# Linear attention and two squared-ReLU FFNs on one core: weights at multiples of 512 bytes, activations 64 bytes past one

## Chip, cores and metric

One core of a Trainium2 chip runs one program. The time is the device time of an execution in microseconds; of a kernel it is the median of its runs. The profiled execution is one more run, with its own time.

## What is computed

The reference, cut to its core. Everything is float32, with 8 x 576 = 4,608 tokens, 8 heads of 64, a model width of 512 and a hidden width of 2,048:

```python
q_s = exp(q - q.max(-1)); q_s = q_s / (q_s.sum(-1) + 1e-9)          # over the head's 64 columns
k_s = exp(k - k.max(2));  k_s = k_s / (k_s.sum(2) + 1e-9)            # over the 576 positions
kv = einsum('bhsd,bhse->bhde', k_s, v)
x = einsum('bhsd,bhde->bhse', q_s, kv)                               # laid out as [4608, 512]
x = square(maximum(x @ moe_w_in, 0)) @ moe_w_out
y = square(maximum(x @ moe2_w_in, 0)) @ moe2_w_out
```

## The kernel before, in words

The tokens are cut into nine blocks j of 512. TensorE works through four phases, each over all nine blocks before the next begins.

Phase 0 (up to 514 us): the attention gives x of a block, transposed, in four tiles [128, 512] (`x_mm`, lines 360 to 368), and `h_mm` (line 383) multiplies it by w_in of the first FFN. A product is done in float32r with both operands split into a high and a low part, three passes for each (`passes`, line 400; the matmul is line 404). A chunk of 128 hidden columns takes 4 x 3 = 12 matmuls of 128x128 weights by 512 columns; a block has 16 chunks.

Phase 1 (514 to 874 us), `second_mm` with l = 0 (line 461): the second product of the first FFN. It is done in the seven products of a Strassen scheme: `combine` (line 641) makes of a tile of weights or of activations seven linear combinations of its quarters, on VectorE and GpSimd (`comb_add`, lines 82 to 86), splits them into a high part on ScalarE (line 92) and a low part on VectorE (line 97), and puts both into one tile [128, 2, 7, 256]. A step a (eight to a block) takes seven products by two halves by three passes, 42 matmuls of 256 columns, with one tile of weights W and one of activations G.

Phase 2 (874 to 1247 us), `first_mm` (line 413): the first product of the second FFN in the same scheme, 84 matmuls of 256 columns for each of four units u of a block, with two tiles W and two tiles x.

Phase 3 (1247 us to the end), `second_mm` with l = 1: as phase 1, but `left, right = (w, g) if l == 0 else (g, w)` (line 466) turns the operands round. `nc.tensor.matmul(ps, a, b)` loads a (128 columns, LDWEIGHTS in the profile) and streams b. So in phases 0 to 2 the weights are loaded and the activations stream; in phase 3 G is loaded and W streams.

Each matmul of line 404 loads weights of its own, and the load for the next matmul runs while the present one streams.

SBUF is divided into places. A tile belongs to a tag, a tag has one buffer (`tile_pool(name="sb", bufs=1)`, line 53), and tiles of one tag follow each other in it. The tags that the change touches are w0 to w7 and hl0 to hl3, each 14 x 256 float32 (14,336 bytes) in every partition:

- w0 to w4 hold in phase 0 three chunks each of the split w_in (line 701: `w0_rooms`), with the chunks f = 0 to 2 in w0, 3 to 5 in w1 and so on. The last chunk, f = 15, lies in hl3. From phase 1 on, w0 to w7 hold the eight tiles W of a phase: step a uses w((a + 5) mod 8) (`slot_of`, line 719). In phase 2 unit u uses two of them.
- hl0 and hl1 hold in phase 0 three of the four tiles x of even and of odd blocks; the fourth lies in hl3 (line 827). In phases 1 and 3, G of step n = 8j + a lies in hl((n + 1) mod 3) (line 947), but for the last steps, which use two places. In phase 2 the two tiles x of a block lie in hl3 and hl0 or in hl1 and hl2.

All slices that a matmul takes of these tiles begin at multiples of 512 bytes from the tile's start.

The order of the work on each engine is fixed before the program is built: `schedule` (line 556) runs a model of the five engines with estimated costs and due times, and the steps are issued in the order that it gives. It knows tags, not addresses. Where a tag lies is settled by the order in which the tags first get a tile: the pool puts them one behind another, rounded up to 32 bytes, from byte 1,152 of a partition.

Of the kernel before, what the change touches and what calls it, by code (L numbers as in the profile page):

```python
# [8 lines left out]
F32 = mybir.dt.float32  # L9
# [11 lines left out]
P = 128  # L21
NP = H // 2
TB = 512
HB = TB // 2
# [17 lines left out]
def linear_attention_two_relu2_ffn(ctx: ExitStack, tc: tile.TileContext, q0, k0, eye, qh, kh, vh, wio, out):  # L42
# [10 lines left out]
    pool = ctx.enter_context(tc.tile_pool(name="sb", bufs=1))  # L53
    psum = ctx.enter_context(tc.tile_pool(name="ps", bufs=1, space=bass.MemoryType.PSUM))
    dram = ctx.enter_context(tc.tile_pool(name="dr", bufs=1, space=bass.MemoryType.DRAM))

    def f32(ap):
        return ap.bitcast(F32)
# [1022 lines left out]
```

## Time and profile before

| | |
|---|---|
| median of 3 runs | 1610.74 us (1606.44 to 1611.1) |
| the profiled execution's own time | 1609.91 us |
| its span, first to last instruction | 1608.1 us |
| TensorE busy (matmul) | 1558.7 us, 97% |
| VectorE busy | 1210.4 us, 75% |
| ScalarE busy | 960.7 us, 60% |
| GpSimd busy | 414.3 us, 26% |
| mean granted clock of TensorE | 0.989 |
| matmuls of line 404, 512 columns in phase 0 | 1,728 |
| matmuls of line 404, 256 columns in phases 1 to 3 | 3 x 3,024 |

A busy share says that an engine has something in flight, not that it works at its best: matmuls are pipelined, and the 280 or so ns that the profile gives for one are the time from its start to its end, of which more than half overlaps the next. What a matmul costs is the distance from its start to the next start. In a stretch in which TensorE is busy from end to end, that is the stretch divided by the number of matmuls.

### The profile page before, as it was taken

What the parts mean: (1) busy time and instruction counts of PE and PEld (TensorE: products, weight loads), DVE (VectorE), ACT (ScalarE), POOL (GpSimd) and SP (SyncE); (2) the same over time, 40 slices, a digit from 0 to 9 for tenths busy, and PEclk for the clock granted to TensorE, in tenths of its full rate; (3) what the DMA queues carried; (4) which work ended last, traced back from release to release, by engine and by line L of the source; (5) the groups of instructions that cost most, each with busy time, mean ns of one, the idle gap of its engine ahead of it and who ended that gap; (6) DMA issues with size and microseconds to landing.
All of it is one profiled execution on the core that took longest, in us unless ns stands there. A gap on an engine that the chain in (4) does not pass through costs nothing. (4 is left out here: it accounts for less than half of the span.)

```text
span 1608.1 us, 29959 instructions
## 1 busy us (share of the span) xinstructions
PE 1558.7 (97%) x11664; PEld 1458.2 (91%) x11664; DVE 1210.4 (75%) x1758; ACT 960.7 (60%) x1605; POOL 414.3 (26%) x329
## 2 busy tenths in 40 slices
PE   5889999999999999999999899999999999999998
PEld 4668887778888999999999899999999999999998
DVE  7887886777632988888889854544337999999986
ACT  7666775666643655555556677777668543434432
POOL 1000000000013333333322243333311533333332
PEclk9899999999999999999999899999999999999999
DMA  8536775677655333333334466665335443333332
GB/s 320 166 119 220 243 252 187 224 240 226 196 183 176 139 132 130 133 132 132 131 111 157 162 214 192 207 207 175 131 132 190 152 144 136 134 134 136 132 118 80
DMA packets 139135, 270.50 MB, mean 168 GB/s; under 512 B 12144, under 2 KB 71664, under 8 KB 138992
## 3 DMA queue, kind: packets, MB, share of 16 engines
q1 hardware_dynamic: 138992, 268.58, 50.3%
q8 instruction: 91, 1.49, 0.4%
q14 instruction: 52, 0.43, 0.1%
HBM read 161.58 MB, written 106.95 MB: 167 GB/s over the span
## 5 line engine op out<-in xcount | busy, mean ns | idle before, releaser
L404 PE MATMUL h<-hl,w 128*128 128x512 f32 x1620 | 399.3, 401 | 13.2 <-DVE w L64 12.1
L404 PEld LDWEIGHTS h<-hl,w 128*128 128x128 f32 x1620 | 305.4, 191 | 84.6 <-DVE w L64 10.9
L404 PE MATMUL m<-x,W 128*128 128x256 f32 x3024 | 362.5, 283 | 6.7 <-DVE W L97 6.4
L404 PEld LDWEIGHTS m<-x,W 128*128 128x128 f32 x3024 | 361.4, 190 | 7.5 <-DVE W L97 7.0
L404 PE MATMUL y<-W,G 128*128 128x256 f32 x3024 | 355.7, 280 | 4.6 <-DVE G L97 4.6
L404 PE MATMUL y<-G,W 128*128 128x256 f32 x3024 | 358.6, 281 | 1.2 <-DVE G L97 1.2
L404 PEld LDWEIGHTS y<-G,W 128*128 128x128 f32 x3024 | 358.2, 189 | 1.7 <-DVE G L97 1.6
L404 PEld LDWEIGHTS y<-W,G 128*128 128x128 f32 x3024 | 354.6, 188 | 5.4 <-DVE G L97 4.6
L92 ACT ACTIVATE G<-hl 128x512 fp32r<-128x512 f32 (+1 forms) x106 | 93.3, 888 | 139.1 <-PE y L404 104.3
L97 DVE TENSOR_TENSOR G<-hl,G 128x512 fp32r<-128x512 f32 (+1 forms) x106 | 128.7, 1218 | 17.8 <-ACT G L92 17.7
L391 ACT ACTIVATE r<-h 128x512 f32<-128x512 f32 x144 | 85.3, 594 | 74.7 <-PE h L404 69.9
L434 POOL TENSOR_TENSOR ts<-ts,ts 128x512 f32<-128x512 f32 x53 | 79.7, 1504 | 183.4 <-ACT ts L431 171.0
L443 DVE TENSOR_TENSOR t<-m,ts 128x512 f32<-128x512 f32 x72 | 49.4, 689 | 100.3 <-PE m L404 89.1
L258 POOL PARTITION_ALL_REDUCE m<-m x28 | 23.4, 836 | 348.2 <-DVE m L254 155.0
L449 ACT ACTIVATE t<-t 128x512 f32<-128x512 f32 x144 | 90.3, 631 | 3.6
L97 DVE TENSOR_TENSOR G<-cf,G 128x1280 fp32r<-128x1280 f32 x51 | 84.8, 1662 | 4.4 <-ACT G L92 4.1
L97 DVE TENSOR_TENSOR G<-att,G 128x1280 fp32r<-128x1280 f32 x50 | 82.2, 1644 | 6.0 <-ACT G L92 5.8
L92 ACT ACTIVATE G<-qd 128x512 fp32r<-128x512 f32 x40 | 25.3, 632 | 80.8 <-PE y L404 59.0
L92 ACT ACTIVATE G<-cf 128x1280 fp32r<-128x1280 f32 x51 | 64.5, 1265 | 14.7 <-DVE cf L84 11.6
L92 ACT ACTIVATE G<-att 128x1280 fp32r<-128x1280 f32 x50 | 63.2, 1265 | 16.1 <-DVE att L84 16.0
L92 ACT ACTIVATE G<-qc 128x512 fp32r<-128x512 f32 x41 | 25.9, 632 | 76.1 <-PE y L404 69.3
L476 POOL TENSOR_TENSOR t<-t,t 128x512 f32<-128x512 f32 x34 | 62.9, 1870 | 30.1 <-DVE t L443 30.1
(166 smaller groups left out, 1988.2 us busy)
## 6 DMA issues: line engine op xcount, KB each, us to landing
g<-r SPq DMA_DIRECT2D x144, 256.0 KB, 3.3
g<-t SPq DMA_DIRECT2D x144, 256.0 KB, 2.7
hl<-g SPq DMA_DIRECT2D x63, 512.0 KB, 3.6
raw<-wio SPq DMA_DIRECT2D x48, 512.0 KB, 5.1
qc<-g SPq DMA_DIRECT2D x41, 512.0 KB, 3.6
qd<-g SPq DMA_DIRECT2D x40, 512.0 KB, 3.6
y<-t SPq DMA_DIRECT2D x72, 256.0 KB, 2.2
w<-wf SPq DMA_DIRECT2D x48, 256.0 KB, 5.0
```

The source lines that it names most:

```text
L92: nc.scalar.activation(out=hls[key][:, 0, r], in_=src, func=AF.Copy)
L97: nc.vector.tensor_tensor(out=hl[:, 1, r], in0=src, in1=f32(hl[:, 0, r]), op=ALU.subtract)
L258: nc.gpsimd.partition_all_reduce(m[:, 1, :P], m[:, 0, :P], P, bass.bass_isa.ReduceOp.max)
L391: nc.scalar.activation(out=r0[j, f].rearrange("p a b -> p (a b)"), in_=m.pop(("h", j, f)), func=AF.Relu)
L404: nc.tensor.matmul(ps, a, b, start=start, stop=True, skip_group_check=True)
L434: nc.gpsimd.tensor_tensor(out=t[k, "s5"], in0=t[k, "s5"], in1=t[k, "s2"], op=ALU.add)
L443: nc.vector.tensor_tensor(out=temp(k, q), in0=m[k, i], in1=t[k, "s5"], op=ALU.add)
L449: nc.scalar.activation(out=t[k, q], in_=t[k, q], func=AF.Square)
L476: nc.gpsimd.tensor_tensor(out=t[k, q], in0=t[k, q], in1=t[k, o], op=ALU.add)
```

## The change

Before any other tile is asked for, the pool is asked for one tile of each of fourteen tags in a fixed order, which settles where these tags lie. Nothing writes or reads these first tiles. The lines behind move down by eight (line 404 becomes 412).

```diff
     pool = ctx.enter_context(tc.tile_pool(name="sb", bufs=1))
     psum = ctx.enter_context(tc.tile_pool(name="ps", bufs=1, space=bass.MemoryType.PSUM))
     dram = ctx.enter_context(tc.tile_pool(name="dr", bufs=1, space=bass.MemoryType.DRAM))
+
+
+    pool.tile([P, 224], F32, name="margin", tag="margin")
+    for tag in [f"w{i}" for i in range(8)]:
+        pool.tile([P, 14 * HB], F32, name=f"{tag}_room", tag=tag)
+    pool.tile([P, 16], F32, name="margin2", tag="margin2")
+    for tag in [f"hl{i}" for i in range(4)]:
+        pool.tile([P, 14 * HB], F32, name=f"{tag}_room", tag=tag)
```

Where the built programs put the places, in bytes from the start of a partition, with the remainder by 512:

| place | before | mod 512 | after | mod 512 |
|---|---|---|---|---|
| w0 | 116,416 | 192 | 2,048 | 0 |
| w1 | 155,392 | 256 | 16,384 | 0 |
| w2 | 175,936 | 320 | 30,720 | 0 |
| w3 | 9,344 | 128 | 45,056 | 0 |
| w4 | 23,680 | 128 | 59,392 | 0 |
| w5, w6, w7 | 38,112, 52,448, 66,784 | 224 | 73,728, 88,064, 102,400 | 0 |
| hl0 | 100,032 | 192 | 116,800 | 64 |
| hl1 | 190,272 | 320 | 131,136 | 64 |
| hl2 | 213,824 | 320 | 145,472 | 64 |
| hl3 | 136,896 | 192 | 159,808 | 64 |

The other places move as well: the eight 2,048-byte places of the evictions from 192 or 256 to 128 or 192 past a multiple of 512, qc and cf from 320 to 256, att2 from 352 to 288, qd from 128 to 64. The instructions of all five engines, their order and their waits are the same, row for row.

## Rows read from the trace of the kernel before

**Rows 1.** The page's head and its first part.
```profile
span 1608.1 us, 29959 instructions
...
PE 1558.7 (97%) x11664; PEld 1458.2 (91%) x11664; DVE 1210.4 (75%) x1758; ACT 960.7 (60%) x1605; POOL 414.3 (26%) x329
```

**Rows 2.** The page's second part: busy tenths in 40 slices of some 40 us.
```profile
PE   5889999999999999999999899999999999999998
...
DVE  7887886777632988888889854544337999999986
...
PEclk9899999999999999999999899999999999999999
```

**Rows 3.** Waits of ScalarE from 1300 to 1590 us: total, times, longest.
```profile
ACT G L92 <- PE y L404: 100.0, 36, 4.4
```

**Rows 4.** Timeline of TensorE, opening of phase 3: start, length, count, idle before.
```profile
1297.72 2.52 PE L404 MATMUL y<-W,G 128*128 128x256 f32 x19 [1.57 <-DVE G L97]
```

**Rows 5.** Stretches of phase 1: length, TensorE busy, matmuls, clock, DMA share, GB/s.
```profile
690.54:695.57 5.03, 5.03 (x44) 1.00 0.41 134
695.57:700.52 4.95, 4.95 (x44) 1.00 0.51 175
705.57:710.33 4.76, 4.76 (x44) 1.00 0.32 110
710.33:715.28 4.95, 4.95 (x44) 1.00 0.34 121
```

**Rows 6.** Stretches of phase 3, the same view.
```profile
1435.68:1440.45 4.78, 4.78 (x44) 1.00 0.41 148
1440.45:1445.21 4.76, 4.76 (x44) 1.00 0.36 120
...
1464.97:1469.92 4.94, 4.94 (x44) 1.00 0.58 202
1469.92:1474.94 5.02, 5.02 (x44) 1.00 0.21 65
1474.94:1479.89 4.95, 4.95 (x44) 1.00 0.42 147
1479.89:1484.65 4.76, 4.76 (x44) 1.00 0.34 119
```

**Rows 7.** Stretches of phase 0, one chunk each, the same view.
```profile
295.47:298.27 2.80, 2.80 (x14) 1.00 0.86 222
473.08:475.80 2.72, 2.72 (x13) 1.00 0.70 215
481.32:484.12 2.80, 2.80 (x13) 1.00 0.48 113
486.92:489.71 2.79, 2.79 (x13) 1.00 0.23 86
500.79:503.54 2.75, 2.75 (x13) 1.00 0.27 105
```

**Rows 8.** Tile G from 1300 to 1590 us: nanoseconds least/median/most, first and last start.
```profile
L97 DVE TENSOR_TENSOR G<-cf,G x20: 1475/1489/2206, 1303.2 to 1580.2; 128x1280 fp32r<-128x1280 f32 x20
...
L97 DVE TENSOR_TENSOR G<-att,G x20: 1477/1487/2206, 1309.9 to 1585.2; 128x1280 fp32r<-128x1280 f32 x20
```

**Rows 9.** Stretches by engine: length, busy (count) of PE, PEld, DVE, ACT, POOL, clock, DMA.
```profile
530.00:860.00 330.00, 330.00 (x2788) 330.00 (x2788) 287.78 (x311) 193.53 (x217) 110.08 (x89) 1.00 0.38 132
...
1247.00:1300.00 53.00, 48.36 (x406) 47.58 (x405) 50.27 (x59) 25.55 (x30) 29.27 (x14) 1.00 0.49 150
1300.00:1590.00 290.00, 290.00 (x2481) 290.00 (x2480) 261.12 (x273) 116.47 (x132) 103.29 (x79) 1.00 0.38 130
```

**Rows 10.** Stretches of phase 2: two blocks, and one of hl3, hl0 with w3, w4.
```profile
1041.82:1121.20 79.38, 79.38 (x674) 1.00 0.61 193
1077.10:1081.34 4.24, 4.24 (x38) 1.00 0.31 103
```

## The prediction, made before the changed kernel ran

> **What bounds the kernel now.** I read the head of the page first: the span is 1608.1 us and TensorE is busy for 97% of it [rows 1]. The slices then show where that holds: from the fourth slice on TensorE stands at 9 with one 8 in the middle, its clock is granted in full nearly throughout, and the only engine near it is VectorE, at 8 and 9 through much of the second quarter and nearly all of the last [rows 2]. In phase 3 the feeders wait for TensorE and not the reverse: ScalarE sat 100.0 us idle, 36 times, until a matmul had released a place hl [rows 3]. Only at the opening of phase 3 does TensorE wait for VectorE's G, in stalls such as 1.57 us [rows 4]. So the time is, to first order, the number of matmuls times the distance between two starts, and the question is whether that distance depends on where the operands lie.
>
> It does, already in the kernel before. Call D the start of the moving operand minus the start of the weights that are loaded next, modulo 512 bytes; within a tile all operands of the three FFN phases and of phase 0 start at multiples of 512 bytes, so D is a property of the two places. In phases 1 and 3 one pair of places is used for 42 matmuls on end, and the stretches in the rows run from the first start of one pair to the first start of the next (a count of x44 holds the two neighbours that overlap the edges). The clock is 1.00 in all of them and TensorE is busy from end to end, so nothing but the pair differs. Phase 1 [rows 5]: hl0 with w0 (D 0) takes 5.03 us, hl1 with w1 (D 64) 4.95, hl0 with w3 (D 64) 4.76, hl1 with w4 (D 192) 4.95. Per matmul that is 119.8, 117.8, 113.4 and 117.8 ns. Phase 3, where the weights move and G is loaded [rows 6]: w3 past hl0 (D 448) 4.78 us, w4 past hl1 (D 320) 4.76, w1 past hl0 (D 64) 4.94, w2 past hl1 (D 0) 5.02, w3 past hl2 (D 320) 4.95, w4 past hl0 (D 448) 4.76.
>
> Three things are to be seen. D 0 is dear. D 448 is cheap each time. D 64, 192 and 320 have two paces, 113.4 and 117.8 ns, that do not mix within a stretch; the cheap D 320 stretch follows a D 448 stretch, the dear one a D 0 stretch, as if each stretch kept the phase in which it found the two reading streams. For 512 columns (phase 0) the order is another [rows 7]: chunks of 12 matmuls take 2.72 us at D 0, 2.75 at D 64, 2.79 at D 384, 2.80 at D 448, and at D 64 once 2.80 as well.
>
> The Trainium skill says otherwise: "TensorE: Matmul & The Clock Gate", part 2, step 1, gives TensorE two independent SBUF read ports and says that loading the next weights takes no read bandwidth from the running matmul. By that sentence alone the change is worth nothing and the time stays at 1610; [rows 5, 6], where the same 42 matmuls differ by 0.27 us with their places, do not agree with it.
>
> **What the change does.** Nothing is added, removed or moved in any queue: row for row the five engines get the same instructions with the same waits. Only the bytes change. All weights come to D-neutral multiples of 512 and all hl places to 64 past one, so D becomes 64 in phases 0 to 2 and 448 in phase 3, for every pair (the one exception is the sixteenth chunk of phase 0, whose weights lie in hl3: D 0 as now in every other block).
>
> Do the other engines feel the new places? VectorE's and ScalarE's do not show it: the 1280-element subtraction has a minimum and median of 1475 and 1489 ns out of cf and 1477 and 1487 out of att [rows 8], two sources and two destinations at different offsets; the spread above that is waiting for the port shared with GpSimd. I take their change as nothing. For transfers I take nothing too; they hide behind TensorE (DMA share 0.38 in phases 1 and 3 [rows 9]).
>
> **The sum, phase by phase.**
> - Phase 3, opening 53 us: TensorE is busy 48.36 and VectorE 50.27 of 53.00 us [rows 9]. VectorE limits here; a faster matmul only waits longer. Gain 0.
> - Phase 3, rest: 290.00 us hold 2,479 matmuls (2,481 with the edges) [rows 9], 117.0 ns each. At D 448 two stretches give 4.78 and 4.76 us per 42, 113.5 ns. From 1300 us to the end there are about 2,590: 2,590 x 3.5 = 9.0 us gained. Cover: VectorE's 261.12 busy us must now fit in 281, that is 93% instead of 90%. It fits on the mean, so I charge nothing.
> - Phase 1: 330.00 us hold 2,786 [rows 9], 118.4 ns. At D 64 the bounds are 113.4 and 117.8; three of the four stretches of D 64 shown (4.95 and 4.94 us of [rows 5, 6], and 4.24 us for 36 matmuls, 117.8 ns, in phase 2 [rows 10]) are dear, so I take 117.8: 0.6 x 2,900 = 1.8 us.
> - Phase 2: 79.38 us for 672 matmuls of two blocks [rows 10], 118.1 ns; at 117.8: 0.3 x 3,024 = 1.0 us.
> - Phase 0: even blocks now have chunks at D 0, 448, 384 and 64, odd ones at 128, 64, 0 and 192; the differences without a row I put at 2.79, near D 384. At 2.75 everywhere an even block gains 3 x (-0.03 + 0.05 + 0.04) = 0.2 us, an odd one 0.3; nine blocks make 2.0 us.
>
> Sum: 9.0 + 1.8 + 1.0 + 2.0 = 13.8 us. The profiled execution took 1609.91 us, 0.8 below the median of the runs shown; 1609.9 - 13.8 = **1596 us**, 0.9% faster.
>
> **The rivals.**
> 1. Phases 1 and 2 fall into the cheap pace. With one D throughout there is no change of pair to throw them out of it again, so the pace that the first matmuls find may hold for a whole phase. Worth 4.4 ns x 2,900 = 12.8 us in phase 1 and 4.4 x 3,024 = 13.3 in phase 2: 1583 with one of them, 1570 with both. For it: the 4.76 us stretch at D 64 [rows 5]. Against it: the dear ones are more, also outside the rows. Chance 0.32 (0.20 one, 0.12 both).
> 2. VectorE becomes the bound of phase 3. It is at 90% and 8 to 9 in the slices; if its bursts at the block ends reach TensorE, half of the 9.0 us stays: 1600 to 1603. Chance 0.07.
> 3. The places do not matter in themselves: the two reading streams never meet, and the differences between the stretches belong to something that comes with the pair, the step's place in the block for instance. Then 1610. Against it: the same hl0 is cheap and dear with other weights, and w4 with hl1 took 4.95 us in phase 1 and 4.76 in phase 3 [rows 5, 6]. With the case that the tiles don't come to lie as said: chance 0.06. It is what the sentence of the Trainium skill quoted above would make of the time.
> 4. Slower: the pace hangs on the absolute offset too, and eight weight places that all begin at the same offset, as none does now, bring each load onto the line that the running matmul reads, as at D 0. Then 119.8 ns holds throughout: phase 1 +1.4 x 2,900 = 4.1, phase 2 +1.7 x 3,024 = 5.1, phase 3 +2.8 x 2,590 = 7.3, and phase 0 at 2.80 for each of 144 chunks, against a mean of 2.765 by the chunks of the sum above, +5: 1631. It decides if D 448 in phase 3 no longer gives 4.76. Against it: pairs with the same D at different offsets agree (w2 past hl1 and hl0 with w0, 5.02 and 5.03 [rows 5, 6]). Chance 0.03.
>
> **How the numbers follow.** Forecast 0.52, rivals 0.32, 0.07, 0.06, 0.03. A measurement of this kernel tells about 0.3% (4.8 us) from no change, so faster means under 1606: forecast, rivals 1 and 2, 0.91; same 0.06; slower 0.03. The range goes from both phases cheap, 1570 less 2 for the scatter of runs, to the weak end of rival 2 with 1 us of scatter: 1568 to 1604. It leaves out rivals 3 and 4.
>
> **What would show it.** In phase 3 after its opening, 42 matmuls take 4.76 to 4.78 us whatever the pair, with ScalarE still waiting for TensorE; in phases 1 and 2 every 42 take the same time, 4.95 us (forecast) or 4.76 (rival 1); chunks of phase 0 take 2.75 us. VectorE's and ScalarE's durations stay. The forecast is wrong if the stretches of phase 3 still differ with the pair, if the phases 1 and 2 leave 113.4 and 117.8 for a third pace, or if TensorE's waits for G grow by more than 4 us.

## The result, and the profile after

The changed kernel took **1592.29 us** (median of 15 runs, 1579.56 to 1605.15) where the kernel before took 1607.22 on the same chips (15 runs, 1602.88 to 1611.1): a ratio of 0.9896, 95% interval 0.988 to 0.9911. The ratios in this document leave out runs more than 1.5% above the fastest of the same kernel (here the two at 1605), so they are not the quotients of the medians. Forecast were 1596 us, 0.9% faster, within 1568 to 1604.

The 15 runs do not scatter evenly. Two lie at 1580 and 1581 us, eleven at 1590.1 to 1593.9, two at 1605. The profile that came with the result is of the first group (1581.43 us), so it shows more gain than the median has. Its head, the counterpart of [rows 1]:

```profile
span 1579.6 us, 29959 instructions
...
PE 1530.1 (97%) x11664; PEld 1431.3 (91%) x11664; DVE 1212.8 (77%) x1758; ACT 963.1 (61%) x1605; POOL 424.6 (27%) x329
```

The instructions are the same 29,959. TensorE is busy for 28.6 us less; VectorE's and ScalarE's busy times differ by 2.4 us, GpSimd's by 10.3. Where TensorE's time went is seen from the groups of its matmul line, which give the first and last start of each phase. First the kernel before (phases 1, 2, 3; nanoseconds from start to end of one, least/median/most, then first to last start in us):

```profile
L404 PE MATMUL y<-G,W x3024: 274/281/388, 514.5 to 874.0; 128*128 128x256 f32 x189
L404 PE MATMUL m<-x,W x3024: 273/281/583, 874.1 to 1247.0; 128*128 128x256 f32 x189
L404 PE MATMUL y<-W,G x3024: 274/280/388, 1240.1 to 1602.6; 128*128 128x256 f32 x189
```

and the same groups after (the line is now L412):

```profile
L412 PE MATMUL y<-G,W x3024: 276/276/388, 509.0 to 853.7; 128*128 128x256 f32 x189
L412 PE MATMUL m<-x,W x3024: 276/279/582, 853.9 to 1226.3; 128*128 128x256 f32 x189
L412 PE MATMUL y<-W,G x3024: 276/276/420, 1219.5 to 1573.9; 128*128 128x256 f32 x189
```

Phase 1 went from 359.5 to 344.7 us, phase 2 from 372.9 to 372.4, phase 3 from 362.5 to 354.4. Phases 1 and 3 have the median of 276 ns throughout, phase 2 has 279: phase 2 runs at the dear pace. The stretches of 42 matmuls say so directly. The view is that of [rows 5 to 7] with TensorE alone (length, busy and count, granted clock, DMA share, GB/s): a chunk of phase 0, two stretches of phase 1 and 24 matmuls near its end, one stretch of phase 2, two of phase 3.

```profile
481.60:484.35 2.75, 2.75 (x13) 1.00 0.21 80
509.99:514.93 4.94, 4.94 (x44) 1.00 0.92 294
526.20:530.96 4.76, 4.76 (x44) 1.00 0.50 172
845.57:848.39 2.83, 2.83 (x26) 1.00 0.03 6
1041.41:1046.36 4.95, 4.95 (x45) 1.00 0.75 205
1440.39:1445.15 4.76, 4.76 (x44) 1.00 0.60 204
1445.15:1449.91 4.76, 4.76 (x44) 1.00 0.14 46
```

Only two paces are left, 4.76 us (113.4 ns per matmul) and 4.95 us (117.8), and the 5.03 of D 0 is gone. But both stand at the same D = 64 in phases 1 and 2, and phase 1 contains both: it begins at 117.8, changes to 113.4 at its 98th matmul, and ends at 117.8 again (2.83 us for 24). The timeline shows what happens at the first change (start, length, count, idle time before and its releaser):

```profile
518.82 1.85 PE L412 MATMUL y<-G,W 128*128 128x256 f32 x14
521.00 3.22 PE L412 MATMUL y<-G,W 128*128 128x256 f32 x26 [0.33 <-DVE G L105]
```

TensorE stands still for 0.33 us, waiting for G, and comes out of it at the other pace. The starts that follow lie 113 or 114 ns apart, those ahead 117 to 119, and this holds for the next 323 us, whatever place the operands come from. At 844.99 us the trace has a shorter wait for G (0.2 us), and the last 9 us of the phase have 117.8 ns once more. What came with a single stall of a third of a microsecond is worth some 12.5 us (2,850 matmuls by 4.4 ns).

ScalarE still waits for TensorE in phase 3 and not the reverse (the counterpart of [rows 3], from 1300 to 1570 us):

```profile
ACT G L100 <- PE y L412: 89.8, 35, 4.1
```

VectorE's work on G has kept its duration (the counterpart of [rows 8], 1300 to 1560 us):

```profile
L105 DVE TENSOR_TENSOR G<-att,G x19: 1476/1484/2214, 1299.7 to 1557.6; 128x1280 fp32r<-128x1280 f32 x19
```

### The profile page after: what moved, and what is told of

The parts are those of the page before. It is cut to its first block, busy times and chain, and to the rows that moved or that the text cites. A ratio compares the mean times of both kernels' runs of the same rounds, so it can differ in the third digit from the quotient of the medians.

```text
span 1579.6 us, 29959 instructions
## 1 busy us (share of the span) xinstructions
PE 1530.1 (97%) x11664; PEld 1431.3 (91%) x11664; DVE 1212.8 (77%) x1758; ACT 963.1 (61%) x1605; POOL 424.6 (27%) x329
## 5 line engine op out<-in xcount | busy, mean ns | idle before, releaser
L412 PE MATMUL h<-hl,w 128*128 128x512 f32 x1620 | 392.9, 397 | 13.4 <-DVE w L72 12.6
L412 PEld LDWEIGHTS h<-hl,w 128*128 128x128 f32 x1620 | 302.5, 189 | 81.4 <-DVE w L72 11.4
L412 PE MATMUL m<-x,W 128*128 128x256 f32 x3024 | 361.2, 281 | 7.6 <-DVE W L105 6.6
L412 PEld LDWEIGHTS m<-x,W 128*128 128x128 f32 x3024 | 360.2, 190 | 8.4 <-DVE W L105 7.3
L412 PE MATMUL y<-W,G 128*128 128x256 f32 x3024 | 347.1, 277 | 5.1 <-DVE G L105 5.1
L412 PEld LDWEIGHTS y<-W,G 128*128 128x128 f32 x3024 | 345.7, 189 | 6.2 <-DVE G L105 5.1
L412 PE MATMUL y<-G,W 128*128 128x256 f32 x3024 | 344.5, 276 | 0.5 <-DVE G L105 0.3
L412 PEld LDWEIGHTS y<-G,W 128*128 128x128 f32 x3024 | 343.8, 188 | 1.2 <-DVE G L105 1.1
L105 DVE TENSOR_TENSOR G<-hl,G 128x512 fp32r<-128x512 f32 (+1 forms) x106 | 132.4, 1253 | 8.4 <-ACT G L100 8.4
```

The source lines that it names most:

```text
L105: nc.vector.tensor_tensor(out=hl[:, 1, r], in0=src, in1=f32(hl[:, 0, r]), op=ALU.subtract)
L412: nc.tensor.matmul(ps, a, b, start=start, stop=True, skip_group_check=True)
```

## The experiments

Two questions were open: whether the distance D is really what sets the pace (and not the absolute offset, the other engines' traffic or the step's place in the block), and what decides between the two paces that one D can have. In the first three kernels the instructions and their order are those of the changed kernel; only margins differ.

### All places at the same multiple of 512 bytes

```diff
-    pool.tile([P, 16], F32, name="margin2", tag="margin2")
```

> The second margin is left out, so weights and activations both begin at multiples of 512 bytes and D is 0 in every phase. Theory (the distance D between the moving operand and the next weights, modulo 512, sets the pace): 42 matmuls of phases 1 to 3 take 5.02 to 5.04 us (119.8 ns each) after their openings, chunks of phase 0 2.72 to 2.75 us, and the kernel is slower than the one before, 1615 to 1625 us. Rival (weights at multiples of 512 bytes are what helps, because a load of 512 bytes then crosses no 512-byte boundary): the weights lie as in the changed kernel, so the time stays at 1580 to 1605 us. Rival (places don't matter): 1607 us.

Measured: 1622.31 us (four runs, 1620.38 to 1624.82), ratio 1.0105, interval 1.009 to 1.012. One stretch of 42 matmuls in each of phases 1, 2 and 3:

```profile
700.00:705.04 5.04, 5.04 (x45) 1.00 0.32 104
1059.98:1065.03 5.05, 5.05 (x45) 1.00 0.50 163
1499.99:1505.03 5.04, 5.04 (x44) 1.00 0.49 157
```

120.0 ns per matmul everywhere, with no second pace. So it is not the common offset of the weights that makes the changed kernel faster, but the 64 bytes between weights and activations: the two kernels lie 30 us apart.

### The same distance the other way round

```diff
-    pool.tile([P, 224], F32, name="margin", tag="margin")
+    pool.tile([P, 160], F32, name="margin", tag="margin")
...
-    pool.tile([P, 16], F32, name="margin2", tag="margin2")
+    pool.tile([P, 112], F32, name="margin2", tag="margin2")
```

> The second margin is 448 bytes instead of 64, the first is 256 bytes shorter to make room: D is 448 in phases 0 to 2 and 64 in phase 3. Theory (D sets the pace): phase 0 loses, 2.79 to 2.80 us a chunk instead of 2.75 (some 6 us more than the changed kernel); phases 1 and 2 take 113.4 ns per matmul if D 448 always ends in the cheap pace, as it did in the kernel before, so some 13 us less each where the changed kernel had 117.8; phase 3 takes 117.8 or 113.4 by its entry. Sum 1575 to 1590 us. If both paces hold at D 448 as well as at D 64, phases 1 to 3 each choose by their entry and the times scatter between 1573 and 1612. Rival (alignment of weights to 512): the gain is gone, 1607 us.

Measured: 1585.61 us (four runs, 1583.6 to 1594.36), ratio 0.9886, interval 0.9857 to 0.9915; the profiled run took 1594.36. One stretch each of phases 1, 2 (D 448) and 3 (D 64):

```profile
699.97:704.91 4.94, 4.94 (x44) 1.00 0.34 106
1040.03:1044.79 4.76, 4.76 (x44) 1.00 0.73 215
1450.02:1454.96 4.94, 4.94 (x44) 1.00 0.34 115
```

Phase 1 is dear at D 448, phase 2 cheap, phase 3 dear at D 64. D 448 is therefore not the cheap distance as such, as [rows 6] had suggested: 64 and 448 share the same two paces, and what differs is which one a phase ends up with. The expectation that D 448 always ends cheap failed in phase 1. In phase 0 the mean distance rose from 229.3 to 233.1 ns, so 512 columns have an order of their own.

### The same distance, other offsets

```diff
-    pool.tile([P, 224], F32, name="margin", tag="margin")
+    pool.tile([P, 176], F32, name="margin", tag="margin")
```

> The first margin is 192 bytes shorter: weights 320 and activations 384 past a multiple of 512, D as in the changed kernel (64, and 448 in phase 3). Theory (only D counts): the same times as the changed kernel, 1579 to 1606 us with one or two clusters, every phase at 113.4 or 117.8 ns. Rival (the multiples of 512 count): the gain is gone or halved, 1600 to 1607 us, with other paces than these two.

Measured: 1593.09 us (ten runs, 1581.29 to 1605.13), ratio 0.9914, interval 0.9889 to 0.994. It has the median of the changed kernel and its three groups as well (two runs at 1581 and 1583, two above 1603). The profiled run (1582.82 us) has phase 1 cheap, phase 2 dear, phase 3 cheap, as the change has. The absolute offset plays no part that can be seen.

### Distances by themselves

A kernel of matmuls alone (it computes nothing of the reference): bursts of 84 matmuls of 256 columns, each with its own weight load in the order of a step, behind a stall, for D = 0 to 480 in steps of 32, six bursts each; then 36 matmuls of 512 columns.

```python
xv = x[:, d // 4:d // 4 + N]     # the moving operand d bytes past the place of the weights
```

> No attention and no FFN is computed here: 84 matmuls of 256 columns in the order of phase 1, on one place of weights and one of activations, with D taken through 0, 32 to 480, six times over, each burst after a stall of another length; then 36 matmuls of 512 columns for D 0, 64 to 448, three times. Theory: with 256 columns D 0 takes 119.8 ns per matmul, 128 and 384 118.7, 64, 192 and 320 either 113.4 or 117.8 by the entry, 448 113.4; offsets of 32 past these lie between; with 512 columns 226.7 ns at D 0, 228.9 at 64, 233 at 448. Rival (what differs is the other engines' traffic in the full kernel, which comes with the pair): here with next to no other traffic all D take the same.

Measured, stretches of 42 matmuls at D 0, 32, 64, 96, 128 and 192, then of 12 matmuls of 512 columns at D 0, 64 and 192:

```profile
31.40:36.44 5.04, 5.04 (x45) 1.00 0.00 0
218.39:223.29 4.90, 4.90 (x44) 1.00 0.01 3
53.30:58.25 4.95, 4.95 (x45) 1.00 0.01 3
64.27:69.31 5.04, 5.04 (x45) 1.00 0.00 0
75.29:80.28 4.99, 4.99 (x45) 1.00 0.00 0
97.09:102.03 4.94, 4.94 (x44) 1.00 0.00 0
1093.27:1095.99 2.72, 2.72 (x13) 1.00 0.00 0
1102.16:1104.91 2.75, 2.75 (x14) 1.00 0.03 6
1120.24:1123.04 2.80, 2.80 (x14) 1.00 0.00 0
```

The DMA engines are idle here and no other engine works beside the bursts, and still D alone moves a matmul from 116.7 ns (D 32 in five of six bursts, the sixth took 117.8) to 120.0 (D 0, and D 96 as well). Every D takes the same values as D + 256, so the period is 256 bytes, not the 512 of the prediction: D 64 equals 320, and 192 equals 448. For 512 columns it is 226.7 ns at D 0, 228.9 at 64, 233.5 at 128 and 233.4 at 192. D 0, the dearest for 256 columns, is the cheapest for 512. The weights stay at one place here; that the distance counts and not the activations' own offset rests on the kernel moved as a whole above, and on [rows 5, 6], where D 0 costs the same at two offsets. The cheap pace of 113.4 ns did not appear in any of the 96 bursts, so a stall by itself does not bring it.

### Breaks of the rhythm

The same kernel, with D = 64 and 192 only, and the 27th and 57th matmul of a burst disturbed: cut into two pieces, or read at another D.

```python
for lo, hi in ((0, v), (v, HB)) if kind == "cut" else ((0, HB),):
    nc.tensor.matmul(banks[i][:, s, lo:hi], wv[:, a, LEFT[i], c], x[:, o + lo:o + hi], start=start, stop=True, skip_group_check=True)
```

> A kernel of matmuls alone (its output is not the reference's): bursts of 84 matmuls of 256 columns, each with its own weight load, at D = 64 and D = 192, each burst behind a stall of TensorE. All distances in a burst are D but at its 27th and 57th matmul, where the rhythm is broken on purpose: either one matmul is cut in two pieces of v and 256 - v columns (v = 16 to 240 in steps of 16, two bursts each), or one or two matmuls read their moving operand at another D (0 to 224 in steps of 32). No other engine works on SBUF beside them. Theory A (the order of weight loads and moving reads is kept until something breaks the rhythm, and what breaks it sets which of two orders follows): the bursts begin at 117.8 ns per matmul as in the sweep, some cuts end in 113.3 to 113.6 ns for all matmuls behind them, in both bursts of that v, others leave 117.8. Theory B (the pace of 113.4 ns in the full kernels comes from what other engines and transfers do at the time of the stall, not from the rhythm of TensorE): no break turns 117.8 into 113.4; all bursts stay at 117.8 ns behind their breaks. Theory C (the pace is drawn by chance at every break): the two bursts of the same v differ, and 113.4 appears without regard to v.

Measured: the two paces exist without any other engine. One burst at D 192, cut at 112 columns: 20 matmuls ahead of the first cut, 20 between the cuts, 20 behind the second.

```profile
260.22:262.49 2.27, 2.27 (x23) 1.00 0.00 0
263.42:265.77 2.35, 2.35 (x22) 1.00 0.00 0
266.94:269.21 2.27, 2.27 (x23) 1.00 0.02 7
```

113.5, 117.5, 113.5 ns: the cut turned the pace, and the next cut turned it back. Both bursts of that v did the same, as did both with v = 176. That refutes theory B (nothing beside TensorE is needed) and speaks against C at D 192. At D 64 it was otherwise: of 30 cut bursts 29 began at 117.8 and one at 113.3, three more turned to 113.3 at their first cut (v = 80, 160, and 64 in its second burst), and these did not repeat in the other burst of the same v. At D 192, 29 of 30 began at 113.3, where the sweep had begun at 117.8 each time. Between the two studies the bursts ahead differ: here the burst before mostly had the same D and left 113.3, there it had another D. So what ran before the stall seems to count as well; this is argued, and it is not the whole: at D 192, of four bursts that followed one of the same D left at 117.8 ns, three began at 113.3. The breaks by another D turned the pace both ways, and none of the eight values did so in every place.

### Cuts tried from the dear pace

```python
turn = ("cut", 112)
run(192, 3, {20: turn, 40: ("cut", cut), 60: turn, 80: ("cut", cut), 100: turn})
```

> A kernel of matmuls alone (its output is not the reference's), in bursts of 126 (three rounds of 42) at D = 192, and others at D = 64. In the study of breaks, a matmul cut at 112 columns turned the pace at D = 192 at each of four places, from 113.3 to 117.8 ns at the first break and back at the second. Here a cut at 112 stands at the 21st, 61st and 101st matmul of each burst, and the cut under test at the 41st and 81st, with 16 to 240 columns in steps of 16, so that each is tried behind 117.8 ns. At D = 64 two matmuls in a row are cut at v, at three places of a burst. Theory A (what breaks the rhythm sets which of two orders follows): the cut at 112 turns 113.3 into 117.8 each time it finds 113.3, and for D = 192 some cuts v end at 113.3 from either pace, in both bursts of that v: those are usable in a kernel. Theory C (each break draws the pace by chance): the two bursts of a v differ in more than a few places.

Measured, the first burst with v = 128: ten matmuls ahead of and behind each of the five cuts.

```profile
142.12:143.30 1.18, 1.18 (x12) 1.00 0.00 0
144.58:145.71 1.13, 1.13 (x12) 1.00 0.00 0
146.97:148.10 1.13, 1.13 (x12) 1.00 0.00 0
149.38:150.56 1.18, 1.18 (x13) 1.00 0.00 0
151.82:152.95 1.13, 1.13 (x12) 1.00 0.00 0
154.23:155.40 1.17, 1.17 (x12) 1.00 0.00 0
```

117.8 ns at the start; the cut at 112 makes it 113.4; the cut at 128 leaves it so; the cut at 112 makes it 117.8; the cut at 128 makes it 113.4; the last cut at 112 makes it 117.8. The second burst of v = 128 gave the same six paces, and in 13 of the 15 pairs the two bursts agree in this way (the pairs of 16 and 32 began at different paces). Wherever the cut at 112 found 113.4 it left 117.8. Found at 117.8, it gave 113.4 at its first place each time and mostly not at the later two, so the place in the round counts too. The cuts at 32, 128, 144, 192 and 208 ended at 113.4 to 113.6 from either pace, if both studies are taken together. At D 64 no pair of cuts brought 113.4 in any of 14 bursts. Theory A holds at D 192, with the reserve that a cut must be known with its place; for D 64 none of these cuts is a handle.

### The changed kernel a second time

> The changed kernel once more, for a second profile of it: its times lie in groups (two runs at 1580 and 1581 us, eleven at 1590 to 1594, two at 1605), and the profile that came with the result is of 1581.43 us, with phase 1 and phase 3 at 113.5 ns per matmul and phase 2 at 117.6. Theory A (each phase keeps one of two paces, decided at its opening, and a phase of 3,024 matmuls at 117.8 ns in place of 113.4 is 13 us longer): a run at 1590 to 1594 us shows two of the phases 1 to 3 at 117.6 to 117.8 and one at 113.4 to 113.6, with lengths that differ by 12 to 13 us in that one phase and by under 2 us in the others. Theory B (the groups come from elsewhere, as from the granted clock or from transfers that come late): the profile shows the same paces as before, and the 11 us lie in gaps or in a stretch of a lower clock.

Measured: 1597.89 us. The phases:

```profile
L412 PE MATMUL y<-G,W x3024: 276/279/388, 513.8 to 871.7; 128*128 128x256 f32 x189
L412 PE MATMUL m<-x,W x3024: 276/279/420, 871.9 to 1243.2; 128*128 128x256 f32 x189
L412 PE MATMUL y<-W,G x3024: 276/276/415, 1236.4 to 1590.3; 128*128 128x256 f32 x189
```

Phase 1 took 357.9 us instead of 344.7, phase 2 371.3 (372.4 in the first profile), phase 3 353.9 (354.4): theory A, 13.2 us in the one phase that was dear this time. Its median is 279 ns here and 276 there. But the two runs are 16.5 us apart, and the rest has another cause, which the expectation had put down to theory B: phase 1 begins 4.8 us later (513.8 against 509.0). That comes about at two places of phase 0. Here is this run first, in two stretches and the wait ahead of the second one's slow part, then the first profile in the same stretches:

```profile
60.00:90.00 30.00, 23.11 (x99) 0.85 0.31 107
255.00:285.00 30.00, 28.09 (x144) 0.89 0.68 221
266.21 0.51 PE L412 MATMUL h<-hl,w 128*128 128x512 f32 x1 [1.50 <-ACT hl L69]
60.00:90.00 30.00, 23.03 (x124) 0.94 0.35 115
255.00:285.00 30.00, 28.87 (x160) 1.00 0.74 231
```

In both stretches more of this run was granted at 1.2 GHz. The first leaves it 1.5 us behind at 120 us. In the second, TensorE waited 1.50 us for hl where it had waited 0.41, the granted clock then fell, and the lag grew from 1.5 us at 259 us to 5.5 at 278. The kernel before has the first stretch as this run has it (0.85, 99 matmuls) and the second at 1.00. Without the 4.8 us this run would have taken 1593.1 us, inside the large group. So the groups are read thus: phases 1 and 3 cheap, 1580; phase 3 alone, 1590 to 1594; none of them, 1605. The first rests on one profile, the second on this one with 4.8 us taken off, the third is argued and not profiled.

The stall that turned phase 1 in the first profile comes here too, and did not turn it:

```profile
524.91 1.68 PE L412 MATMUL y<-G,W 128*128 128x256 f32 x12 [0.95 <-DVE G L105]
526.91 4.28 PE L412 MATMUL y<-G,W 128*128 128x256 f32 x34 [0.33 <-DVE G L105]
```

The second stall is as long as that of the first profile (0.33 us, again ahead of the 98th matmul), but another of 0.95 us lies 12 matmuls ahead of it, which the first profile has not. So the length of a stall does not settle the pace behind it; what does, stays open.

### Places chosen from the studies

D = 192 in phases 1, 2 and 3, where 113.4 ns is what most of the cuts left, and D = 0 mod 256 in phase 0. As the operands change sides in phase 3, G lies 128 bytes further there than in phase 1.

```diff
-    pool.tile([P, 224], F32, name="margin", tag="margin")
+    pool.tile([P, 96], F32, name="margin", tag="margin")
...
-    pool.tile([P, 16], F32, name="margin2", tag="margin2")
+    pool.tile([P, 48], F32, name="margin2", tag="margin2")
     for tag in [f"hl{i}" for i in range(4)]:
-        pool.tile([P, 14 * HB], F32, name=f"{tag}_room", tag=tag)
+        pool.tile([P, 14 * HB + 32], F32, name=f"{tag}_room", tag=tag)
...
-            hls[key] = pool.tile([P, 2, 7, HB], F32R, name=key, tag=tag)
+            room = pool.tile([P, 14 * HB + 32 * (tag[:2] == "hl")], F32R, name=key, tag=tag)
+            lo = 32 * (tag[:2] == "hl" and (key[:3] == "G1_") != (int(tag[2]) % 2))
+            hls[key] = room[:, lo:lo + 14 * HB].rearrange("p (a b n) -> p a b n", a=2, b=7)
...
+        lo += (16, 48)[int(place.tag[2]) % 2] if place.tag[:2] == "hl" else 0
```

> Places chosen by the studies: D = 192 mod 256 in phases 1, 2 and 3 (where the matmuls alone mostly took 113.4 ns after a stall, and D = 64 nearly always 117.8), and D = 0 mod 256 in phase 0 (226.7 ns per matmul of 512 columns in the sweep, 228.9 at D = 64). Instructions and order are unchanged. From the profiled run of the change (1581.4 us; phases 475.3, 344.7, 372.4 dear, 354.4 us): phase 0 gives 1590 x (229.3 - 226.7) ns = 4.2 us, a cheap phase 2 another 13 (359.1 as in e2_turned). Theory A (D decides how likely the cheap pace is at each opening): all phases cheap 1564 us, one phase dear 1577; the median lies between these, and some runs at 1564. Theory B (the pace of a phase is drawn at its opening, whatever of the two D stands there): the groups of the change, moved by 4 us: 1576, 1588 and 1601, with most runs at 1588. Phase 0 settles both ways at 226.7 ns, or the sweep does not carry over to a kernel with other traffic.

Measured: 1574.93 us (six runs, 1567.55 to 1596.67; ratio to before 0.979, interval 0.9765 to 0.9816). The profiled run (1567.55 us):

```profile
L414 PE MATMUL y<-G,W x3024: 276/276/387, 509.1 to 853.7; 128*128 128x256 f32 x189
L414 PE MATMUL m<-x,W x3024: 276/276/420, 853.9 to 1213.5; 128*128 128x256 f32 x189
L414 PE MATMUL y<-W,G x3024: 276/276/385, 1206.6 to 1560.1; 128*128 128x256 f32 x189
```

All three phases have the cheap median: phase 2 takes 359.6 us where the first profile of the change had 372.4. Phase 0 settles at 226.8 ns in its last fifth, and its mean is 227.9 (229.3 in the change), which would be half of the 4.2 us expected; but phase 1 begins at 509.1 us as in the change (509.0), so in this profile none of it shows in the time. The runs lie at 1567.6, 1568.1 and 1570.8, then 1579.1, 1579.3 and 1596.7: that fits theory A, and its second half too, that a phase can still come out dear, though the later runs were not profiled. None lies at the 1588 us that theory B gave to most.

### One matmul cut now and then

```diff
+    KICKS = (2, 6, 12, 24, 36, 48, 60)
...
+                if cut and not start:
+                    nc.tensor.matmul(ps[:, :P], a, b[:, :P], start=False, stop=True, skip_group_check=True)
+                    nc.tensor.matmul(ps[:, P:], a, b[:, P:], start=False, stop=True, skip_group_check=True)
+                    cut = False
+                else:
+                    nc.tensor.matmul(ps, a, b, start=start, stop=True, skip_group_check=True)
```

A matmul of product i = 2 is cut in the steps named; phase 2 has half as many steps, so there are 7 + 4 + 7 = 18 cuts.

> The places of e8_places, and in each of phases 1, 2 and 3 one matmul cut into two of 128 columns in the 3rd, 7th, 13th, 25th, 37th, 49th and 61st step (21 in all). At D = 192 a cut at 128 left 113.4 ns in every burst of the two studies of breaks, from either pace. A cut costs about 115 ns (58 + 113 + 170 ns where two matmuls take 227), so 2.4 us in all. Theory A (the pace is a state of the rhythm of loads and reads, which this cut sets): all three phases run at 113.3 to 113.6 ns behind their first cut in every run, the runs lie together at 1564 + 2.4 = 1566 us, within 1563 to 1571, with no group 12 us above. Theory B (other traffic decides in the kernel): the groups of e8_places remain, 2.4 us later, and dear stretches stand behind cuts in the profile.

Measured: 1572.77 us (five runs, 1567.12 to 1574.85), ratio 0.9784, interval 0.9768 to 0.98: above the expected 1563 to 1571, and within the interval of the kernel without cuts. No run lies more than 8 us above the lowest, where three of six lay 11.5 us or more above it without the cuts; with so few runs it is not shown that the cuts did this. What a cut can do in the full kernel is seen at the opening of phase 3, where the phase had come out dear: 20 matmuls ahead of the cut at 1219.59 us, and 20 behind it.

```profile
1217.12:1219.47 2.35, 2.35 (x22) 1.00 1.03 327
1220.29:1222.56 2.27, 2.27 (x22) 1.00 0.81 246
```

117.5 ns and 113.5, at a DMA share of 1.0, with no idle time between. It did not last: the four stalls from 1245.5 to 1264.2 us left 117.8, 113.3, 117.8 and 113.3, and the next cut came later. Another cut, at 881 us in phase 2, came right behind a stall and left 117.8; the next stall turned it. The first cut of phase 1, at 518.6 us, lies between two stalls, so what turned that phase can't be told. The other cuts left 113.3 where that pace had held before, one of them right behind a stall. So theory A, that the first cut of a phase sets its pace, fails in phases 2 and 3. Three of the five runs are 6 to 9 us above the expected 1566; phase 0 moved by nearly as much between the changed kernel's two profiles, but these runs were not profiled, so their cause stays open. Against the kernel before, this version is 2.2% faster; the ratios of the two give 0.9784 / 0.9896 = 0.989 against the change.

## Why the prediction was right

The sum, term by term, in us against the profiled run of before (spans 1608.1, 1579.6 and 1596.1):

| term | predicted | first profile of the change | second profile |
|---|---|---|---|
| opening and phase 0 | -2.0 | -5.5 | -0.7 |
| phase 1 | -1.8 | -14.8 | -1.6 |
| phase 2 | -1.0 | -0.5 | -1.6 |
| phase 3 | -9.0 | -8.1 | -8.6 |
| span | -13.8 | -28.5 | -12.0 |

- **The bound.** "The number of matmuls times the distance between two starts" was right: the longest waits of the matmul line, 12.6 us for w of phase 0, 6.6 for W of phase 2 and 5.4 for G, were 12.1, 6.4 and 5.8 before, and phases 1 to 3 moved by their matmul distance.
- **Phase 3.** 113.4 ns throughout after the opening, as taken from [rows 6]; the opening gave nothing, as taken from [rows 4, 9]. The step that was weak is why: the stretches of D 448 were read as "D 448 is cheap". It is one of two paces that D 448 can have (dear in phase 1 of the turned layout). The trace of before could not tell this: all 14 stretches at D 448 in its phases 1 and 3 are cheap. Its pairs repeat every 24 steps, but for the last four, so the same step of the sequence has the same past each time: hl0 with w3 in phase 1 (D 64) is cheap at steps 14, 38 (the row at 705.57 in [rows 5]) and 62:

```profile
586.24:591.00 4.76, 4.76 (x44) 1.00 0.29 110
```

The other stretches of D 64 in phase 1, at other steps, are dear each time. That the largest term, 9.0 us, came out at 8.1 to 8.6 is thus luck as far as the reason given goes: phase 3 came out of its opening at the cheap pace in both profiles, and the two runs at 1605 are probably those where it did not.
- **Phases 1 and 2.** The two bounds, 113.4 and 117.8, were both right, and there was no third pace. Taking the dear one for both gives the large group. The second profile agrees with both terms to 0.6 us. But the dear one was chosen by counting stretches, three against one, and not by a reason; phase 1 was cheap in the first profile and dear in the second with the same instructions.
- **Phase 0.** Chunks of 2.75 us, as forecast, save the sixteenth. The distance between its matmuls, where no wait lies between, fell from 231.1 to 229.3 ns in the mean, some 3 us for 1,728, where the term said 2.0. The rest is mostly the granted clock, which the sum did not contain: 1.6 of the 5.5 us that the first profile gained were there by 120 us, and the second lost 4 of its own in the stretch behind 266 us.
- **Rival 1** happened, with one phase, in 2 of 15 runs (chance given for one phase 0.20), and both phases cheap in none; its time of 1583 us was met by 1580 and 1581. Only the run of 1581 was profiled. Its mechanism was right in that a pace is kept through changes of the pair, and wrong in "the pace that the first matmuls find": the first 97 matmuls of phase 1 had 117.8 ns, and a stall changed it.
- **Rival 2** did not happen: TensorE's waits for G are 5.4 us after and 5.8 before, and VectorE is busy for 245.7 of 270 us in the body of phase 3, 91%.
- **Rival 3** is refuted by the layout with D 0 (1622 us with the same instructions) and by the sweep, where nothing else moves. (That "nothing but the pair differs" in [rows 5, 6] was too strong: the DMA share there goes from 0.21 to 0.58. In the rows of the sweep it is at most 0.03.) The sentence that it rested on, of the Trainium skill, "TensorE: Matmul & The Clock Gate", part 2, step 1, on two independent read ports, does not agree with these runs: the same load beside the same matmul takes 116.7 to 120.0 ns in the sweep by D alone, and 113.3 where the cheap pace is found.
- **Rival 4** named a price that exists, 119.8 ns throughout, but for equal places, not for this layout; equal offsets of the weights did not cost it by themselves. Its picture of a load on the line that the running matmul reads is shown by no run.

What the prediction missed is the spread: it gave the runs 1 or 2 us of scatter inside a case, and a run of this kernel can have either of two paces in each of three phases, 13 us apiece, plus 5 us by the granted clock in phase 0. It also had the period of D as 512 bytes, where the sweep shows 256. And it took its 13.8 us from a run of 1609.91 us; from the later median of 1607.22 the same sum gives 1593.4, nearer to the 1592.29 measured.

## What to carry to other kernels

When matmuls follow each other end to end with a weight load each, divide a stretch by its count and compare the pairs of places: a few nanoseconds per matmul that go with the places are worth a margin tile, chosen for the column count in use (D 0 for 512 columns, 32, 64 or 192 mod 256 for 256), and never equal places for 256 (nor places 96 apart). Where one layout shows two paces, look for the stall at which it changes, profile more than one run, and ask what leaves the better one: here a distance of 192. A single matmul cut in two turned the pace with nothing else running and once in the full kernel, but a gain in time from it is not shown. A term that rests on a cheap stretch should say whether the stretch is cheap by its place or by its past.

## What was not expected of the hardware

- One layout has two steady paces, 113.3 and 117.8 ns per matmul of 256 columns at D 64 and 192 (mod 256). Where all pairs have one D, TensorE keeps a pace for hundreds of microseconds, across changes of tile; in the profiles of such kernels it changes only at a stall, at the change from phase 2 to 3, where the two mix, or at a cut. Stalls of equal length, 0.33 us at the same matmul, left 113.3 in one run and 117.8 in another.
- The change is not drawn afresh: at D 192, the two bursts of 13 of 15 pairs went through the same sequence of paces. What kind of state it is, no run here tells.
- The period is 256 bytes, and 512 columns order the distances differently from 256 (226.7, 228.9, 233.5, 233.4 ns at D 0, 64, 128, 192).
- A cut in two halves costs some 115 ns: 58 + 113 + 170 ns for three starts, where two uncut matmuls take 227.
